# Loading the filter of a long convolution: four transfers of 32 rows spread over all partitions, in place of four into 32 partitions each

## The chip, the cores and the metric

The kernel runs on one core of a Trainium2 chip. Its time is the device time of one execution in microseconds, the median of 3 runs: 234.15 us (233.83 to 234.19).

## The reference, cut to what matters

The output is a sum of three terms over a sequence of S = 2048 positions and D = 640 channels, in bf16:

```
xn  = layernorm(A_q)                                  # along the 640 channels
ks  = 4-tap causal shift filter of k, per channel     # taps: shift_k [640, 4]
kv  = ks * v
y   = causal convolution of kv with ssm_k, per channel   # ssm_k [640, 2048], by FFT of length 4096
y   = y + kv * ssm_D                                  # ssm_D [640]
out = A_q + xn * y + (sigmoid(xn @ w_gate) * (xn @ w_up)) @ w_down     # 640 -> 1728 -> 640
```

In the kernel `h` is the filter `ssm_k`, one row of 2048 taps for each channel, and `D` is `ssm_D`. Since `kv * D` is a convolution with a filter that has D at tap 0 alone, the kernel adds D to tap 0 of h.

## The kernel before, in words

The work has two halves that share the engines. The gated unit runs over 4 groups of 512 positions: `gate` and `up` products (L271) into PSUM, sigmoid on ScalarE (ACT, L280), the multiplication with `up` on VectorE (DVE, L286), and the down projection (L315). The convolution runs over 5 chunks of 128 channels. For each chunk it takes kv and h through a two-stage Fourier transform, multiplies them, and goes back through two inverse stages:

- `load_k`, `load_halo`, `load_v`, `load_taps`, `load_h` bring a chunk in. k with its halo goes to `kx`, v to half 0 of the tile `kvh`, the taps (one row, broadcast to all partitions) to `sraw`, from which `taps` (L155) makes `sc`.
- `h_turn` (L334) turns h with two DVE transposes in blocks of 32 x 32 from the tile `hn` into half 1 of `kvh`. `add_D` (L328, GpSimd) adds D at tap 0. `kv_op` (L348 to L357, DVE) makes kv in half 0.
- `st1_mm` (L374, L376) is the first stage on TensorE, with the table `S1t` as weights; ACT or DVE empties PSUM (`st1_ev`), and `wr1` (L392) writes the result to a DRAM tile `d`. `rd2` (L409) reads it back transposed, `st2_mm` (L418), `prod` and `inv1_mm` (L447) follow; `wr2` and `rdb` (L463, L467, L479) go through DRAM again to `bi`; `inv2_mm` (L488) and `inv2_q` (L493, tile `yx`) finish.

The tile `hn` has 128 partitions and 4 x 512 columns. Partition 32q + r, block k holds the q-th quarter (512 taps) of row 32k + r of the chunk: this is the arrangement from which block transposes give time on the partitions. `hn`, `dr`, `sraw` and `yx` have one buffer each, reused from chunk to chunk. `dr` holds the 128 values of D of one chunk in partition 0.

The order of all work is written out by hand: a string of some 900 letters, each taking the next step of one of about 30 chains. No scheduler changes it, so each engine's instructions, and SyncE's (SP's) transfers, stand in that order. SyncE issues all transfers but three. It waits in order: an issue whose buffer isn't free holds up all that follow. Completions are told by eight semaphores, which the transfers use in turn, so a transfer also waits for the one that had the same semaphore before it. In SyncE's queue, h of chunk 0 stands after the weights w_gate and w_up and before v of chunk 0, the second part of w_down and the table S1t; h of chunk 1 after S1t, and before the second group of x (L133), the taps of chunk 1 (L147) and k of chunk 1.

Of the kernel before, what the change touches and what calls it, by code (L numbers as in the profile page):

```python
# [10 lines left out]
BF16 = mybir.dt.bfloat16  # L11
# [3 lines left out]
ALU = mybir.AluOpType  # L15

S = 2048
DM = 640
FF = 1728
P = 128  # L20
# [37 lines left out]
def kernel(  # L58
# [14 lines left out]
    nc = tc.nc  # L73
# [6 lines left out]
    Drow = A_ssm_D.rearrange("(o d) -> o d", o=1)  # L80
# [7 lines left out]
    res = ctx.enter_context(tc.tile_pool(name="res", bufs=1))  # L88
    cv = ctx.enter_context(tc.tile_pool(name="cv", bufs=1))
    dr = ctx.enter_context(tc.tile_pool(name="dr", bufs=1, space=bass.MemoryType.DRAM))  # L90
# [7 lines left out]
    S1t = res.tile([P, NB, 2, P], U16, name="S1t")  # L98
    TBt = res.tile([P, 2, NB, P], U16, name="TBt")
    SMt = res.tile([P, 3, 32], U16, name="SMt")  # L100
    S1 = S1t.bitcast(BF16)
    TB = TBt.bitcast(BF16)
    SM = SMt.bitcast(BF16)
# [21 lines left out]
    sync = nc.sync  # L125
# [3 lines left out]
    cin = [dict() for _ in range(NC)]  # L129
# [5 lines left out]
    def load_h(c):  # L135

        d = cin[c]
        d["hn"] = cv.tile([P, 4, 512], BF16, name="hn")
        d["dr"] = cv.tile([1, P], BF16, name="dr")
        sync.dma_start(d["dr"][:, :], Drow[:, c * P:(c + 1) * P])  # L140
        for q in range(4):
            src = A_ssm_k[c * P:(c + 1) * P, 512 * q:512 * q + 512].rearrange("(k r) t -> r k t", k=4)
            sync.dma_start(d["hn"][32 * q:32 * q + 32, :, :], src)

    def load_taps(c):
        cin[c]["sraw"] = cv.tile([P, 4 * P], BF16, name="sraw")
        sync.dma_start(cin[c]["sraw"][:], srow[:, 4 * c * P:4 * (c + 1) * P].to_broadcast((P, 4 * P)))  # L147

    def taps(c):
# [175 lines left out]

    def add_D(c):
        h0 = cin[c]["kvh"][0:1, 1, 0:2, :].rearrange("p b c -> p (b c)").rearrange("p (c e) -> p e c", e=2)[:, 0, :]
        nc.gpsimd.tensor_tensor(h0, h0, cin[c]["dr"][:, :], ALU.add)  # L328

    def h_turn(c, n):  # L330

# [27 lines left out]
    chunks = [dict() for _ in range(NC)]  # L359
# [6 lines left out]
    def st1_mm(c, n):  # L366
# [5 lines left out]
        for i in range(4):  # L372
            b = 4 * n4 + i
            nc.tensor.matmul(ps[:, i, 0:P], lhsT=S1[:, b, h, :], rhs=cin[c]["kvh"][:, 0, b, :], start=True, stop=True)  # L374
            hp = cin[c]["kvh"][:, 1, :, :].rearrange("p b c -> p (b c)").rearrange("p (b c e) -> p b e c", b=8, e=2)
            nc.tensor.matmul(ps[:, i, P:2 * P], lhsT=S1[:, b, h, :], rhs=hp[:, b // 2, b % 2, :], start=True, stop=True)  # L376

# [21 lines left out]
    def rd2(s):  # L399
# [5 lines left out]
        else:  # L405
            t2 = (xn[:, 12:NB, :].rearrange("p b d -> p (b d)")[:, 0:2048] if at == 2 else
                  S1[:, 8 * at:8 * at + 8, :, :].rearrange("p b h k -> p (b h k)")).rearrange("p (r e) -> p r e", r=8)
        src = chunks[c]["d1"].rearrange("(r q) h b e -> r (q h b) e", q=NQ)
# [60 lines left out]
    def rdb(c, n):  # L469
# [4 lines left out]
        elif c and n == 1:  # L474
            bi = S1[:, 8:NB, :, :].rearrange("p (h b) s c -> p h (b s) c", h=2)
        else:
# [12 lines left out]
                                 start=(h == 0), stop=(h == 1))  # L489

    def inv2_q(c, m):
        chunks[c]["yx", m] = yx = cv.tile([P, 4, P], BF16, name="yx")
        nc.vector.tensor_tensor(yx[:, :, :], chunks[c]["pb", m][:, :, :], xn[:, 4 * m:4 * m + 4, c * P:(c + 1) * P],  # L493
                                ALU.mult)

# [35 lines left out]
    for i in range(4):  # L531
        m = 3 if i < 3 else NC
# [33 lines left out]
    def hs(c):  # L566
        return [(load_h, c)]
# [7 lines left out]
    for k in ((load_w, sync, 512, 1024, 0),  # L575
              (load_w, sync, 512, 1024, 1),
              (load_taps, 0),
              (sync.dma_start, SMt[:], SMd.ap()),
              (load_w, sync, 1024, 1280, 0),
              (load_w, sync, 1024, 1280, 1),  # L580
              (load_wd, sync, 0, 7),
              *ks(0),
              (load_w, sync, 1280, FF, 0),
              (load_w, sync, 1280, FF, 1),
              *hs(0),
              *vs(0),
              (load_wd, sync, 7, NFC),
              (sync.dma_start, S1t[:], S1d.ap()),
              *hs(1),
              (load_x, sync, 1),  # L590
              *ks(1),
              *vs(1)):
        step("m", *k)
# [4 lines left out]
    for c in range(NC):  # L598
        for n in range(2):
            step("H", h_turn, c, n)  # L600
        step("D", add_D, c)
        for n in range(8):
            step("a", st1_mm, c, n)
# [17 lines left out]
        for m in range(4):  # L621
            step("d", inv2_mm, c, m)
            step("q", inv2_q, c, m)
            step("q", inv2_x, c, m)
        for n in range(16):
            step("k", kv_op, c, n)
        if c == 0:
            continue
        step("T", load_taps, c)
        step("t", taps, c)  # L630
        if c > 1:
# [73 lines left out]
```

## Time and profile before

| what | value |
|---|---|
| median of 3 runs | 234.15 us (233.83 to 234.19) |
| the profiled execution's own time | 234.78 us |
| its span, first to last instruction | 233.0 us |
| granted TensorE clock | 1.000 |
| bytes read from and written to HBM | 36.12 MB, 18.35 MB |
| transfers of h | 20 of 128 KB each |
| one h transfer, issue to landing | 3.4 to 7.7 us, median 5.0 |
| SyncE's time for one such issue | 0.31 to 0.43 us, median 0.42 |

How to read the profile: PE is TensorE, PEld its weight loads, DVE VectorE, ACT ScalarE, POOL GpSimd, SP SyncE (SPq its queue, which issues transfers). L143 is line 143 of the kernel before. A line of the timeline holds start and length in us, engine, line, operation, what is written from what, how many instructions, and in square brackets the engine's idle time before it with what ended it. A line of the stages holds the window, its length, busy time and instructions for PE, PEld, DVE, ACT and POOL, the granted clock, the share of the 16 transfer engines' time that packets took (packets overlap a little, so it can exceed 1), and GB/s. In the rows of ten-digit slices a 9 is 90% or more.

### The profile page before, as it was taken

The numbers are of one execution on the slowest core, as the hardware profiler recorded it, in microseconds if no ns is written. First come the engines' busy times: TensorE is split into PE (matmuls) and PEld (weight loads), VectorE is DVE, ScalarE is ACT, GpSimd is POOL, SyncE is SP. The second block draws the span as 40 slices with busy tenths as digits, with TensorE's granted clock in tenths as the row PEclk, the third lists the DMA queues.
The fourth block names the chain that finished last, engine by engine and source line by source line (L and its number), as shares of the span: only waits on it lengthen the run. The fifth ranks groups of instructions, "written<-read, shape, count | busy, mean of one in ns | idle before, by whom it ended". The sixth has DMA issues, their size and how long they took to land.

```text
span 233.0 us, 5431 instructions
## 1 busy us (share of the span) xinstructions
PE 227.5 (98%) x2199; PEld 130.9 (56%) x2200; DVE 203.4 (87%) x357; ACT 123.5 (53%) x158; POOL 12.4 (5%) x26
## 2 busy tenths in 40 slices
PE   7999999997999999999999999999999999999995
PEld 2844446776454555677554544478654544446772
DVE  5444899799999999999999999997799999997773
ACT  2533321676364887765675847674556667752000
POOL 5210010040001100000011000000000000000000
PEclk9999999999999999999999999999999999999999
DMA  6999999896999969999989899689989999364884
GB/s 199 325 329 208 267 317 294 208 266 143 330 221 303 299 221 242 263 223 230 329 237 277 224 319 272 184 217 190 269 210 311 279 263 254 117 169 117 220 266 136
DMA packets 96159, 56.79 MB, mean 244 GB/s; under 512 B 55878, under 2 KB 90374, under 8 KB 95878
## 3 DMA queue, kind: packets, MB, share of 16 engines
q1 hardware_dynamic: 95702, 56.03, 92.6%
q10 hardware_dynamic: 432, 0.41, 0.5%
q8 instruction: 17, 0.28, 0.5%
q14 instruction: 8, 0.07, 0.1%
HBM read 36.12 MB, written 18.35 MB: 234 GB/s over the span
## 4 chain that ended last, share of the span: by engine, by line
PE 87%; DVE 5%; DMA 4%; issue 1%; SPq 1%; ACT 0%; DVEq 0%
PE pu L271 22%; PE pg L271 22%; PE pd L315 21%; PE psb L488 4%; DMA x<-in_A_q_dram 4%; PE ps L374 3%; PE ps L376 3%; PE ps L418 3%; PE psa L447 2%; PE idle L514 2%; PE pg L292 1%; DVE st L200 1%; PE pg L262 1%; PE pu L262 1%; DVE acc L354 1%
## 5 line engine op out<-in xcount | busy, mean ns | idle before, releaser
L271 PEld LDWEIGHTS <-w 128*128 128x128 bf16 x500 | 46.7, 98 | 53.9 <-issue 4.3
L315 PE MATMUL pd<-wd,hT 128*128 128x320 bf16 (+2 forms) x447 | 65.9, 299 | 0.1
L271 PE MATMUL pu<-xnT,w 128*128 128x512 bf16 x250 | 62.2, 379 | 0.0
L271 PE MATMUL pg<-xnT,w 128*128 128x512 bf16 x250 | 62.2, 379 | 0.0
L315 PEld LDWEIGHTS <-hT 128*128 128x128 bf16 x448 | 41.7, 98 | 18.2 <-issue 2.4
L280 ACT ACTIVATE sig<-pg 128x512 bf16<-128x512 f32 x52 | 31.1, 601 | 30.5 <-PE pg L271 23.8
L286 DVE TENSOR_TENSOR hT<-sig,pu 128x512 bf16<-128x512 bf16 x52 | 35.0, 682 | 10.8 <-PE pu L271 6.9
L232 ACT CAST xz<-ps 128x1024 bf16<-128x1024 f32 x36 | 35.1, 1014 | 15.5 <-PE ps L418 15.5
L232 ACT CAST t<-ps 128x1024 bf16<-128x1024 f32 x24 | 23.8, 1012 | 16.7 <-PE ps L376 14.5
L433 DVE TENSOR_TENSOR xz<-xz 128x2048 bf16<-128x2048 bf16 x20 | 24.4, 1221 | 0.2
L374 PE MATMUL ps<-kvh,S1t 128*128 128x128 bf16 x160 | 21.5, 218 | 1.2 <-DVE kvh L357 1.2
L376 PE MATMUL ps<-kvh,S1t 128*128 128x128 bf16 x160 | 21.6, 220 | 0.0
L354 DVE TENSOR_TENSOR acc<-acc,tmp 128x1024 bf16<-128x1024 bf16 x30 | 20.5, 684 | 0.3
L352 DVE TENSOR_TENSOR tmp<-kx,sc 128x1024 bf16<-128x1024 bf16 x30 | 20.5, 682 | 0.3
L320 DVE TENSOR_TENSOR x<-pd,x 128x320 bf16<-128x320 f32 (+2 forms) x32 | 15.2, 484 | 3.8 <-PE pd L315 3.6
L374 PEld LDWEIGHTS <-S1t 128*128 128x128 bf16 x160 | 15.5, 97 | 3.9 <-DVE kvh L357 1.4
L376 PEld LDWEIGHTS <-S1t 128*128 128x128 bf16 x160 | 15.4, 96 | 2.7 <-issue 0.2
L200 DVE BATCH_NORM_STATS2 st<-x 128x6 f32<-128x320 bf16 x32 | 13.8, 473 | 2.3 <-DMA x<-in_A_q_dram 2.3
L232 ACT CAST TBt<-ps 128x1024 bf16<-128x1024 f32 x14 | 13.8, 1012 | 2.7 <-PE ps L376 2.7
L493 DVE TENSOR_TENSOR yx<-psb,xn 128x512 bf16<-128x512 f32 x20 | 13.7, 687 | 1.4 <-PE psb L488 0.8
L431 DVE STREAM_SHUFFLE xz<-xz 128x512 f32<-128x512 f32 x20 | 14.6, 729 | 0.0
L232 ACT CAST ao<-psa 128x1024 bf16<-128x1024 f32 x9 | 9.0, 1013 | 8.6 <-PE psa L447 6.9
(56 smaller groups left out, 159.2 us busy)
## 6 DMA issues: line engine op xcount, KB each, us to landing
t<-d SPq DMA_DIRECT2D x15, 512.0 KB, 6.0
d<-t SPq DMA_DIRECT2D x13, 512.0 KB, 4.1
d<-TBt SPq DMA_DIRECT2D x7, 512.0 KB, 5.9
d<-ao SPq DMA_DIRECT2D x6, 512.0 KB, 5.5
bi<-d SPq DMA_DIRECT2D x6, 512.0 KB, 5.4
kx<-in_A_k_dram SPq DMA_DIRECT2D x10, 256.0 KB, 5.8
hn<-in_A_ssm_k_dram SPq DMA_DIRECT2D x20, 128.0 KB, 5.0
kvh<-in_A_v_dram SPq DMA_DIRECT2D x10, 256.0 KB, 5.2
```

The source lines that it names most:

```text
L200: nc.vector.bn_stats(st[:, i, SD * s2:SD * s2 + SD], x[:, b, s2 * 320:(s2 + 1) * 320])
L232: nc.scalar.copy(out=out, in_=in_)
L271: nc.tensor.matmul(pg[:, :], lhsT=w[:, c, u * UP + fc * P:u * UP + (fc + 1) * P], rhs=xnT[:, :, c, :], start=(c == 0), stop=(c == NC - 1))
L280: nc.scalar.activation(sig[fc][:, :], pgs[0, fc][:, :], ACT.Sigmoid)
L286: nc.vector.tensor_tensor(hT[:, fc, :], sig[fc][:, :], pgs[1, fc][:, :], ALU.mult)
L315: nc.tensor.matmul(pd[:, :], lhsT=hT[:, fc, bb * P:(bb + 1) * P], rhs=wd[:, fc, es], start=(fc == 0), stop=(fc == NFC - 1))
L320: nc.vector.tensor_tensor(x[:, 4 * t + bb, es], pds[bb, half][:, :], x[:, 4 * t + bb, es], ALU.add)
L352: nc.vector.tensor_tensor(d["tmp"][:, :, :], kx[:, lo + 3 - m:hi + 3 - m, :], sb(m), ALU.mult)
L354: nc.vector.tensor_tensor(d["acc"][:, :, :], d["acc"][:, :, :], d["tmp"][:, :, :], ALU.add)
L374: nc.tensor.matmul(ps[:, i, 0:P], lhsT=S1[:, b, h, :], rhs=cin[c]["kvh"][:, 0, b, :], start=True, stop=True)
L376: nc.tensor.matmul(ps[:, i, P:2 * P], lhsT=S1[:, b, h, :], rhs=hp[:, b // 2, b % 2, :], start=True, stop=True)
L433: nc.vector.tensor_tensor(z[:, 1:3, :, :], z[:, 0:1, :, :].to_broadcast((P, 2, 8, P)), z[:, 1:3, :, :], ALU.mult)
```

## The change

Each chunk's h still comes in four transfers of 128 KB, but they are cut the other way. Before, transfer q brings one quarter of the taps of all 128 rows into the 32 partitions of that quarter. After, transfer k brings all 2048 taps of 32 rows into block k of all 128 partitions. Both move 128 pieces of 1024 bytes. On the source side the new transfer steps over q (4), r (32) and 512 taps.

D comes once, 640 values into one row that stays (`Dt`), in place of 128 values a chunk. The room in SBUF for it is made by letting `sraw` and `yx`, which have the same size, share one buffer (`tag="sy"`). Nothing else changes; the engines' instructions and their order are the same.

```diff
+    Dt = res.tile([1, DM], BF16, name="Dt")
...
     def load_h(c):
 
         d = cin[c]
+        if c == 0:
+            sync.dma_start(Dt[:, :], Drow[:, :])
         d["hn"] = cv.tile([P, 4, 512], BF16, name="hn")
-        d["dr"] = cv.tile([1, P], BF16, name="dr")
-        sync.dma_start(d["dr"][:, :], Drow[:, c * P:(c + 1) * P])
-        for q in range(4):
-            src = A_ssm_k[c * P:(c + 1) * P, 512 * q:512 * q + 512].rearrange("(k r) t -> r k t", k=4)
-            sync.dma_start(d["hn"][32 * q:32 * q + 32, :, :], src)
+        for k in range(4):
+            r0 = c * P + 32 * k
+            sync.dma_start(d["hn"][:, k, :], A_ssm_k[r0:r0 + 32, :].rearrange("r (q t) -> q r t", q=4))
 
     def load_taps(c):
-        cin[c]["sraw"] = cv.tile([P, 4 * P], BF16, name="sraw")
+        cin[c]["sraw"] = cv.tile([P, 4 * P], BF16, name="sraw", tag="sy")
...
     def add_D(c):
...
-        nc.gpsimd.tensor_tensor(h0, h0, cin[c]["dr"][:, :], ALU.add)
+        nc.gpsimd.tensor_tensor(h0, h0, Dt[:, c * P:(c + 1) * P], ALU.add)
...
     def inv2_q(c, m):
-        chunks[c]["yx", m] = yx = cv.tile([P, 4, P], BF16, name="yx")
+        chunks[c]["yx", m] = yx = cv.tile([P, 4, P], BF16, name="yx", tag="sy")
```

## The prediction

> **What bounds the kernel now.** I read the page first (shares, slices, chain), then the queue of SyncE in order of time, then who waits around the h loads.
>
> ```profile
> span 233.0 us, 5431 instructions
> ...
> PE 227.5 (98%) x2199; PEld 130.9 (56%) x2200; DVE 203.4 (87%) x357; ACT 123.5 (53%) x158; POOL 12.4 (5%) x26
> ...
> DMA  6999999896999969999989899689989999364884
> ...
> PE 87%; DVE 5%; DMA 4%; issue 1%; SPq 1%; ACT 0%; DVEq 0%
> ```
>
> TensorE is busy nearly throughout and carries 87% of the chain, so a transfer costs time only where its landing holds up TensorE, directly or through DVE or ACT. But the transfer engines have no idle stretch either before 190 us (nines in the DMA row), so extra time there is passed on to what is queued behind. The stages, with the DMA share and GB/s last in each line:
>
> ```profile
> 22.00:30.00 8.00, 8.00 (x39) 3.61 (x38) 6.93 (x11) 2.28 (x4) 0.00 (x0) 1.00 1.12 255
> 30.00:36.00 6.00, 6.00 (x30) 2.71 (x28) 5.93 (x9) 1.79 (x3) 0.78 (x1) 1.00 1.11 352
> 36.00:46.00 10.00, 10.00 (x92) 7.47 (x91) 8.29 (x16) 3.87 (x5) 0.00 (x0) 1.00 0.96 241
> ```
>
> From 22 to 46 us, where the h of chunks 0 and 1 is loaded, the share is about 1: the queue never runs dry. SyncE's order there, and the consumers:
>
> ```profile
> 22.76 1.76 SPq L143 DMA_DIRECT2D hn<-in_A_ssm_k_dram x4
> ...
> 33.67 1.75 SPq L143 DMA_DIRECT2D hn<-in_A_ssm_k_dram x4
> 35.46 1.29 SPq L133 DMA_DIRECT2D x<-in_A_q_dram  x1
> 36.80 0.43 SPq L147 DMA_DIRECT2D sraw<-in_A_shift_k_dram  x1
> ```
>
> ```profile
> 42.79 1.11 DVE L334 STREAM_TRANSPOSE kvh<-hn 128x512 f32<-128x512 f32 x1 [1.15 <-DMA hn<-in_A_ssm_k_dram]
> 44.29 0.89 DVE L200 BATCH_NORM_STATS2 st<-x 128x6 f32<-128x320 bf16 x2 [0.39 <-DMA x<-in_A_q_dram]
> ```
>
> ```profile
> 44.75 0.66 ACT L155 COPY sc<-sraw 128x512 bf16<-128x512 bf16 x1 [1.07 <-DMA sraw<-in_A_shift_k_dram]
> 45.31 1.91 ACT L232 CAST t<-ps 128x1024 bf16<-128x1024 f32 x2
> ```
>
> The reader should see that h of chunk 1, the x group behind it and the taps (sraw) behind that are each awaited already. There is no slack at 42.8 to 44.8 us, and ACT empties PSUM (`t<-ps`) for TensorE's next first-stage matmuls (46.1 us) only after the taps.
>
> **The change, part by part.** The program's order shows the same instructions in the same order on TensorE, DVE, ACT and GpSimd; only SyncE's transfers differ.
>
> *h now.* The four transfers of chunk 0 are issued from 22.76 to 24.09 us and take 4.8 to 5.3 us to land: landings at 27.55, 28.15, 28.73, 29.37, a step of 0.61 us with a full queue. Each is 128 rows of 1024 B, 8 an engine on 16 engines, so 76 ns a row. The weight load of 640 KB (40 rows of 1024 B an engine) landed 1.87 us after the one before it, 47 ns a row. So h now pays 4 x 0.61 = 2.4 us a chunk on all engines, with slow rows. [...]
>
> *h after: how many engines.* The trace records each engine's completion as a semaphore increment. Transfers whose outermost step counts 128, 112, 64 or 32 get 16 landings; the 15-row halo (L164) gets 15, and one increment within 0.2 us of its issue; the D row (L140, one row) gets a single landing. The engines used follow the outermost count. After the change the destination's outermost count is 128, but the source's is 4 (the quarters q; then 32 rows of 512). No transfer here has such a pair; the nearest, the read-back of `bi` (128 against 256), is on 16. The bounds are 4 and 16 engines. I take 4, since a small outermost count has cut the engines each time it occurred. [...]
>
> *Price.* On 4 engines a transfer is 32 rows an engine: 32 x 47 ns = 1.5 us, 6.0 us a chunk, 3.6 us more than now on those four engines (the other twelve get nothing). Bounds: 8 x 47 ns = 0.4 us on 16 engines, 0.8 us a chunk less; or 32 rows at today's 76 ns, 9.7 us a chunk, 7.3 more. I keep 47 ns, the row of transfers into all partitions. Whatever is queued behind waits for its share on the four engines.
>
> *Chunk 0.* Last landing 29.37 + 3.6 = 33.0 us; the DVE transpose L334 started at 30.12, so DVE stands for 2.9 us, with the product L357 and the `up` multiplications L286 behind it, which free PSUM for TensorE. The v load, w_down and S1t (awaited at 40.5 us, landed 39.98) follow in the queue. This isn't added, since the next wait contains it.
>
> *Chunk 1.* With the queue never dry, the 3.6 us of chunk 0 are still there: 7.2 us on four engines. Today one straggling engine sets the landings: x has 15 landings by 42.6 (mean 41.6) and the last at 44.27; h means 39.8 and the last at 42.66; sraw 42.3 and 44.65. If the straggler isn't one of the four, these become 7.2 on top of the means: h 47.0 (+4.3), x 48.8 (+4.5), sraw 49.5 (+4.8). DVE and ACT wait for these with under 0.15 us of slack, and TensorE for ACT. I take **4.5 us**, chunk 0's share included.
>
> *Chunks 2 to 4*, each 3.6 us later against today's slack. Chunk 2: landed 69.42, transpose at 72.14, so 0.9 late; the v half behind it landed 73.57, needed from 75.06, so 2.1 late on DVE. Chunk 3: 92.44 against 96.02, just covered. Chunk 4: 112.14 against 119.68, covered; behind it the write of `d` lands at 116.96 and ACT needs its buffer from 119.2 to 120.6: 0 to 1.4 late. Together 0.9 to some 4; I take **2.4 us**, the middle.
>
> *Issue.* An issue whose sides have different outermost counts (`bi`, L479) took 0.53 us against 0.42 for h: 0.11 x 20 = 2.2 us of SyncE, 0.44 a chunk. Hidden by the backlog; bounds 0 to 0.4. SyncE itself was held in single issues up to 2.67 us (18.36) when some 130 rows an engine were outstanding; the four h transfers now bring 128 on four engines, so what follows is issued later, but it would have waited in the queue anyway: 0.
>
> *D.* Four issues fewer (0.26, 0.23, 0.91, 0.39 us) and no wait for GpSimd before chunk 1 (1.6 us); but h behind it waits for the DVE transpose that ends at 33.64, and started at 33.67 already. 0; at best -0.4. The completion semaphores, eight in turn, are dealt differently: the 1.5 us for which the last h of chunk 2 waited for x falls to the read L409, issued 2 us after that landing: 0.
>
> *sraw and yx in one buffer.* The last copy out of sraw is at 109.5, the first yx (L493) at 145.9: 36 us of cover, 0.
>
> **Sum.** 4.5 + 2.4 = 6.9 us. The profiled execution took 234.78 us (span 233.0 and 1.8 around); so 241.7 beside it, and 234.15 + 6.9 = **241.0** on the median, from which the profiled run stands 0.6 up.
>
> **Rivals.** *1, sixteen engines: not slower.* The rows run at 47 ns and each chunk frees 0.8 us of queue. For it: destination of 128 partitions, and 76 ns now. Against: no transfer in the trace kept 16 engines with a small outermost count. What it could gain is TensorE's 1.2 us wait at 55.2 for DVE, late since 42.79; up to 0.8 of it, less where the straggler sets the landing: 233.3 to 234.3, say 233.7. It decides if an h transfer shows 16 landings. *2, four engines, mostly hidden.* The straggler's 2 to 2.7 us and gaps at 50 us (TensorE and DVE before the transposed loads) absorb all but some 2.5 us: 236.6. Against: the waits under 0.15 us at 42.8 to 44.8. *3, four engines and worse.* Rows at 56 ns, between 47 and 76, make 4 x 32 x 56 ns - 2.4 = 4.8 us a chunk: 9.6 less the 2.7 that the straggler hides (7.2 - 4.5) = 6.9 for the first two chunks, 2.4 + 3 x 1.2 = 6.0 for the rest: 247; a straggler among the four adds 2.0 instead (243 to 249).
>
> **Chances.** Forecast, 5 to 9 us more: 0.50. Rival 1: 0.20, of it 0.07 faster, 0.10 within 0.2% (0.47 us, about what a measurement of this kernel can tell from no change) and 0.03 slower. Rival 2: 0.14. Rival 3: 0.16. The range 233.9 to 248 leaves out the faster part of rival 1 and the end of rival 3, some 0.15; the forecast's own range is 239 to 243. Faster 0.07, same 0.10, slower 0.83.
>
> **What would show it.** Each h transfer with one increment at issue and four landings, and four in a row landing 1.5 us apart; to-landing of h from 5.0 up to 8 or more; the DVE waits before L334 and L200 of chunk 1 grown from 1.15 and 0.39 to some 5 together, ACT's before L155 likewise, and a TensorE gap near 46 us; packets of 1024 B at 47 ns. Wrong, if h shows sixteen landings, or if h lands late and TensorE has no new gap.

## The result and the profile after

| | us, median | runs |
|---|---|---|
| kernel before | 234.34 | 6, from 233.83; one stray run of 336.42 |
| changed kernel | 243.69 | 6, from 243.27 to 246.18 |

The ratio is 1.043 (95% interval 1.037 to 1.049), taken without the stray run; by the medians of the table the changed kernel is 9.35 us slower, 9.5 us without that run. The profiled execution of the changed kernel took 243.77 us, with a span of 242.0 us and a granted clock of 1.000. Line numbers of the changed kernel are those of the kernel before plus 1. The page:

```profile
span 242.0 us, 5426 instructions
...
PE 229.3 (95%) x2199; PEld 131.4 (54%) x2200; DVE 203.5 (84%) x357; ACT 123.2 (51%) x158; POOL 12.5 (5%) x26
...
DMA  6999678899878997889899999969999899654884
...
PE 49%; DMA 22%; SPq 15%; DVE 9%; issue 3%; ACT 2%; DVEq 0%; ACTq 0%
```

The engines do the same work as before (TensorE 229.3 us busy for 227.5, DVE 203.5 for 203.4). TensorE's share of the chain that ended last fell from 87% to 49%; transfers and SyncE's queue now hold 37% of it. The dips in the DMA row are new: the queue has work, but not for all transfer engines. The same three stages as in the prediction (DMA share and GB/s last):

```profile
22.00:30.00 8.00, 8.00 (x39) 3.64 (x38) 6.54 (x12) 2.39 (x4) 0.00 (x0) 1.00 0.73 208
30.00:36.00 6.00, 6.00 (x30) 2.69 (x28) 3.42 (x5) 1.19 (x2) 0.77 (x1) 1.00 0.74 204
36.00:46.00 10.00, 8.40 (x68) 5.68 (x67) 8.53 (x14) 3.21 (x4) 0.00 (x0) 1.00 0.97 270
```

The share was 1.12, 1.11 and 0.96 before. SyncE's order in that stretch is unchanged, but it stands in single issues:

```profile
22.74 3.19 SPq L144 DMA_DIRECT2D hn<-in_A_ssm_k_dram  x4
25.98 4.06 SPq L174 DMA_DIRECT2D kvh<-in_A_v_dram  x2
30.08 2.60 SPq L187 DMA_DIRECT2D wd<-in_B_w_down_dram  x1
...
36.72 2.25 SPq L144 DMA_DIRECT2D hn<-in_A_ssm_k_dram  x4
```

The four issues of h took 1.76 us before, and now 3.19 and 2.25. Chunk 1's begin at 36.72, where they began at 33.67, since the buffer `hn` waits for chunk 0's second transpose. In the semaphore records each h transfer now shows one early increment (0.9 to 1.5 us after its issue begins in sixteen of the twenty, 2.3 to 2.8 in four) and then four landings. From issue to last landing it takes 4.9 to 9.4 us, in the median 6.9. The last landings of chunk 0 are at 28.30, 29.95, 31.37 and 33.06 us, a mean step of 1.59; those of chunk 1 at 41.94, 44.33, 46.36 and 47.79, a mean step of 1.95.

Who waits, in the timelines of DVE, ACT and TensorE:

```profile
33.18 1.10 DVE L335 STREAM_TRANSPOSE kvh<-hn 128x512 f32<-128x512 f32 x1 [2.54 <-DMA hn<-in_A_ssm_k_dram]
...
47.91 1.10 DVE L335 STREAM_TRANSPOSE kvh<-hn 128x512 f32<-128x512 f32 x1 [3.23 <-DMA hn<-in_A_ssm_k_dram]
49.48 0.89 DVE L201 BATCH_NORM_STATS2 st<-x 128x6 f32<-128x320 bf16 x2 [0.46 <-DMA x<-in_A_q_dram]
```

```profile
50.00 0.64 ACT L156 COPY sc<-sraw 128x512 bf16<-128x512 bf16 x1 [4.04 <-DMA sraw<-in_A_shift_k_dram]
50.55 1.92 ACT L233 CAST t<-ps 128x1024 bf16<-128x1024 f32 x2
```

```profile
37.92 1.24 PE L293 MATMUL pg<-xnT,w 128*128 128x512 bf16 x5 [1.60 <-DMA wd<-in_B_w_down_dram]
51.61 0.22 PE L375 MATMUL ps<-kvh,S1t 128*128 128x128 bf16 x1 [2.94 <-ACT t L233]
60.43 0.23 PE L375 MATMUL ps<-kvh,S1t 128*128 128x128 bf16 x1 [1.14 <-DVE kvh L358]
```

The second TensorE line is the chain of the forecast: x and the taps are late, ACT empties PSUM only after the taps, and TensorE stands for 2.94 us before the first-stage matmul. Ahead of it there is a wait of 1.60 us that the forecast had folded into this one. The view puts it down to w_down, but these matmuls don't read w_down. Their matmul instruction waits for DVE's semaphore, and DVE ends a multiplication with `up` at 37.86, 0.05 us before the matmul starts:

```profile
37.19 0.67 DVE L287 TENSOR_TENSOR hT<-sig,pu 128x512 bf16<-128x512 bf16 x1
```

So this wait, too, comes from h of chunk 0: DVE stood 2.54 us for it at 33.18 and reached its multiplications late. The third wait, 1.14 us, is for DVE's product kv, behind the late h of chunk 1. The profile before has such a wait at the same matmul:

```profile
55.24 0.23 PE L374 MATMUL ps<-kvh,S1t 128*128 128x128 bf16 x1 [1.20 <-DVE kvh L357]
```

A comparison of these two profiles therefore doesn't show it. The experiments below left nine other profiles in which chunk 1's h runs on eight or sixteen engines, and none of them has this wait.

To see where TensorE falls behind, its weight loads can be matched one to one between the two profiles. The changed kernel runs 0.4 us late before L293, 2.2 after it, 5.25 at the first-stage matmul at 51.61, and still 5.2 at 111 us. It then loses more at the second-stage matmul L419 (5.9 at 117 us) and at the gate matmul L272 (7.7 at 132 us), and ends 9.0 late. So about 5.2 us are lost by chunks 0 and 1, nothing that shows by chunk 2, and 3.7 us while chunks 3 and 4 come in. Against the profile of the kernel with h alone undone (first experiment below), which has no wait at the third place, the delay is 5.1 us at 51.61 and 6.3 behind 60.43. The profiled execution of the kernel before stood 0.4 us above its median here, and 0.6 to 1.0 above the medians of the larger sets below, so differences against it come out short.

### The profile page after: what moved, and what is told of

It reads as the page before. It is cut to its first block, busy times and chain, and to the rows that moved or that the text cites. A ratio compares the mean times of both kernels' runs of the same rounds, so it can differ in the third digit from the quotient of the medians.

```text
span 242.0 us, 5426 instructions
## 1 busy us (share of the span) xinstructions
PE 229.3 (95%) x2199; PEld 131.4 (54%) x2200; DVE 203.5 (84%) x357; ACT 123.2 (51%) x158; POOL 12.5 (5%) x26
## 4 chain that ended last, share of the span: by engine, by line
PE 49%; DMA 22%; SPq 15%; DVE 9%; issue 3%; ACT 2%; DVEq 0%; ACTq 0%
PE pd L316 16%; PE pu L272 11%; PE pg L272 10%; DMA hn<-in_A_ssm_k_dram 7%; PE psb L489 4%; DMA sraw<-in_A_shift_k_dram 4%; DMA kvh<-in_A_v_dram 3%; DMA kx<-in_A_k_dram 3%; DMA d<-ao 3%; PE ps L419 3%; SPq L178 2%; DMA t<-d 2%; SPq L144 2%; SPq L393 2%; DVE kvh L335 2%
## 5 line engine op out<-in xcount | busy, mean ns | idle before, releaser
L272 PEld LDWEIGHTS <-w 128*128 128x128 bf16 x500 | 46.7, 98 | 55.7 <-issue 6.2
L272 PE MATMUL pg<-xnT,w 128*128 128x512 bf16 x250 | 62.2, 379 | 1.6 <-ACT sig L281 1.6
L272 PE MATMUL pu<-xnT,w 128*128 128x512 bf16 x250 | 62.2, 379 | 0.0
L281 ACT ACTIVATE sig<-pg 128x512 bf16<-128x512 f32 x52 | 31.1, 601 | 30.5 <-PE pg L272 23.3
L335 DVE STREAM_TRANSPOSE kvh<-hn 128x512 f32<-128x512 f32 x10 | 10.9, 1102 | 6.4 <-DMA hn<-in_A_ssm_k_dram 6.4
```

The source lines that it names most:

```text
L272: nc.tensor.matmul(pg[:, :], lhsT=w[:, c, u * UP + fc * P:u * UP + (fc + 1) * P], rhs=xnT[:, :, c, :], start=(c == 0), stop=(c == NC - 1))
L281: nc.scalar.activation(sig[fc][:, :], pgs[0, fc][:, :], ACT.Sigmoid)
L335: nc.vector.transpose(to[:, 4 * n:4 * n + 4, :, :], hv[:, 4 * n:4 * n + 4, :, :])
```

## The experiments

**Which part of the change, and how many engines.** Four kernels on one chip, against 234.03 us of the kernel before (233.46 to 235.62, 25 runs). The first undoes the h part alone and keeps D in one transfer and the shared buffer:

```diff
-        for k in range(4):
-            r0 = c * P + 32 * k
-            sync.dma_start(d["hn"][:, k, :], A_ssm_k[r0:r0 + 32, :].rearrange("r (q t) -> q r t", q=4))
+        for q in range(4):
+            src = A_ssm_k[c * P:(c + 1) * P, 512 * q:512 * q + 512].rearrange("(k r) t -> r k t", k=4)
+            sync.dma_start(d["hn"][32 * q:32 * q + 32, :, :], src)
```

> The changed kernel with h loaded as before (four transfers into 32 partitions each); D in one transfer and the shared buffer of sraw and yx stay. Theory (the loss is all from h on four engines): 233.7 to 234.8 us, the time of before, and sixteen landings for each h transfer. Rival (the other transfers of D, the semaphores dealt differently or the shared buffer carry a part): 235 us or more.

Measured: 234.02 us, ratio 1.0005 (0.998 to 1.003). Each h transfer has sixteen landings again. D in one transfer and the shared buffer cost and bring nothing that can be measured; the loss is h's.

The other three keep a destination of all 128 partitions and pieces of 1024 bytes, and differ from one another in the source's outermost count alone. A transfer of theirs reads 512 taps of 128 rows, where the change reads 2048 taps of 32 rows, and brings them to other partitions, so the filter is not the reference's; the amount of work is the same.

```diff
-            r0 = c * P + 32 * k
-            sync.dma_start(d["hn"][:, k, :], A_ssm_k[r0:r0 + 32, :].rearrange("r (q t) -> q r t", q=4))
+            src = A_ssm_k[c * P:(c + 1) * P, 512 * k:512 * k + 512].rearrange("(b a) t -> a b t", a=16)   # a=8, a=2
+            sync.dma_start(d["hn"][:, k, :], src)
```

Sixteen:

> Each h transfer again fills block k of all 128 partitions with 128 rows of 1024 B, but the source steps over 16 outermost and 8 inner rows (the rows land in other places, so the convolution's filter is not the reference's; the amount of work is the same). Theory (the source's outermost count sets the engines): sixteen landings, 8 rows an engine at about 47 ns, 0.4 us a transfer, 233.3 to 234.4 us. Rival (writing one block of 128 partitions, or a source of two steps, is slow by itself): 240 us or more.

Eight:

> As the kernel with sixteen outermost steps, with 8 outermost and 16 inner rows (the filter's rows again land in other places). Theory: eight landings and one increment at issue; 16 rows an engine at 50 to 58 ns, 0.8 to 0.95 us a transfer against 0.61 before, some 1 us more a chunk on eight engines, most of it under what slack there is: 234.3 to 236.5 us. Rival (count of engines doesn't matter): the same time as with sixteen.

Two:

> As the kernel with sixteen outermost steps, with 2 outermost and 64 inner rows. Theory: two landings and one increment at issue; 64 rows an engine at 50 to 58 ns, 3.2 to 3.7 us a transfer, 13 to 15 us a chunk against 2.4 before and some 6.7 in the changed kernel: some 6 to 8 us more a chunk than the changed kernel, nearly all exposed, 270 to 283 us. Rival (the engines' count doesn't matter): no slower than the changed kernel, 243.7 us.

| source's outermost count | landings of an h transfer | step in chunk 0, us | time, us | ratio (95%) |
|---|---|---|---|---|
| 16 | 16 | 0.46 | 233.65 | 0.997 (0.995 to 0.999) |
| 8 | 8 | 0.96 | 234.38 | 1.002 (0.999 to 1.004) |
| 4 (the change, from the result above) | 4 | 1.59 | 243.69 | 1.043 (1.037 to 1.049) |
| 2 | 2 | 2.90 | 268.24 | 1.146 (1.139 to 1.153) |

The number of engines is the source's outermost count in all four, and it carries the whole loss: with sixteen, the transfer into all partitions is a little better than the kernel before. Its step of 0.46 us is 57 ns a row, above the expected 47. Eight engines take twice as long for an h, and the time still doesn't change: what covers a late h ends between 1.0 and 1.6 us a transfer. With two, step and time came out below what was expected (3.2 to 3.7 us, 270 to 283 us). The 268.24 us are not the price of the engines alone: the granted clock of these four executions was only 0.936 to 0.961. With two engines alone at work, their rate can be read from the GB/s row (slices of 0.8 us from 22 to 54 us):

```profile
GB/s 153 375 372 365 149 36 46 46 45 46 46 45 46 70 227 144 47 116 258 40 69 161 381 395 394 316 379 420 216 46 46 46 46 46 46 46 45 155 243 378
```

46 GB/s on two engines is 23 GB/s each, or 1024 bytes in 45 ns; the step of 2.90 us over 64 rows says the same. That is the price of a row when the other engines are empty.

**Which chunks.** Here some chunks load h as the change does and the others as before (`if c < 2:` and so on around the two loops); D and the buffer are as in the change. The first four kernels ran against 233.79 us of the kernel before (233.44 to 234.81, 7 runs).

> The changed kernel, but chunks 2 to 4 load h as before; only chunks 0 and 1 go in four transfers on four engines. Theory A (the loss comes at two places: TensorE's delay grew by about 5.2 us up to the first-stage matmul L375 of chunk 1, and by 3.7 us after 111 us): 234.0 + 5.2 = 239.2 us, between 238.5 and 240.0, and together with the run of chunks 2 to 4 alone the two losses add up to the 9.3 us of the whole change. Theory B (the two places are one: a late start leaves the later chunks less cover): more than 5.2 is left here or less there, and the two don't add up.

> The changed kernel, but chunks 0 and 1 load h as before; chunks 2 to 4 go in four transfers on four engines. Theory A: 234.0 + 3.7 = 237.7 us, between 237.0 and 238.5, with h of chunk 2 late but TensorE not (in the changed kernel its delay didn't grow there) and the loss at the copy of sraw of chunk 4 (L156) and the gate matmuls behind it. The prediction's step gave 2.4 (236.4). Theory B (the transfers' dates hang on the queue, not on TensorE, so that without the 5.2 us at the start TensorE reaches these loads earlier than they land): 239 or more.

> The changed kernel, but only chunk 0 loads h in four transfers on four engines, the others as before. Theory A (backlog on four engines, carried on in a queue that isn't dry, and covered in part by the one engine that lands 2 to 2.7 us after the others before chunk 1): 3.3 to 4 us of backlog, of which the straggler covers up to 2.7; the wait for w_down at L293 grows from about 0 to 1.6 us as in the changed kernel: 235.3 to 236.2. Rival (no cover, each chunk carries half of the 5.2): 236.6.

> The changed kernel, but only chunk 1 loads h in four transfers on four engines, the others as before. Theory A: 4 us of backlog less the straggler's 2.7: 235.3 to 236.0, the two runs of one chunk together 2 us or more short of the 5.2 of both. Rival (no cover): 236.6, and the two add up.

The run of the last three chunks led to three kernels with one of them each, run against 234.16 us (233.41 to 235.34, 35 runs):

> The changed kernel, but only chunk 2 loads h in four transfers on four engines, the others as before. The prediction's step: DVE 0.9 to 2.1 us late, so 234.7 to 235.9. Rival, from the changed kernel's trace, where TensorE's delay didn't grow at this place: within 0.5 us of the kernel before, 233.6 to 234.4; DVE is late, but does other work before TensorE needs what hangs on it.

> The changed kernel, but only chunk 3 loads h in four transfers on four engines, the others as before. The prediction's step: just covered, 0, so within 0.5 us of the kernel before, 233.5 to 234.4. Rival, from the run of the last three chunks, where TensorE's delay grew by about 1.8 us at 111 to 112 us (L424, for a cast by DVE), before h of chunk 4 was issued: then this comes from chunk 3, 235.3 to 236.0.

> The changed kernel, but only chunk 4 loads h in four transfers on four engines, the others as before. The prediction's step: the write of d behind it lands late, 0 to 1.4 us, so 233.8 to 235.2, and SyncE's being held in issue costs nothing. Rival: SyncE is held in the four issues (4.0 us in the changed kernel against 1.75) and the small transfers of the transforms behind it (the reads t<-d, xn<-d and the writes d<-t), which need no bandwidth but start at once in the kernel before, are late by that and by the rows in front of them on the four engines: 1.8 to 2.5 us, 235.6 to 236.4, with ACT's wait for the write d<-t at 125 us at 3 us or more.

| chunks on four engines | time, us | over before | ratio (95%) |
|---|---|---|---|
| 0 and 1 | 240.40 | 6.6 | 1.028 (1.025 to 1.032) |
| 2, 3 and 4 | 237.94 | 4.15 | 1.016 (1.013 to 1.020) |
| 0 | 236.18 | 2.4 | 1.011 (1.007 to 1.015) |
| 1 | 236.80 | 3.0 | 1.013 (1.010 to 1.016) |
| 2 | 234.63 | 0.5 | 1.002 (1.000 to 1.003) |
| 3 | 236.20 | 2.0 | 1.009 (1.006 to 1.012) |
| 4 | 234.13 | 0.0 | 1.000 (0.998 to 1.003) |

What follows, by theory. Theory A's split stands for the later chunks (237.94 in 237.0 to 238.5). For the first two it was low (240.4 against at most 240.0). The two halves sum to 10.8 against 9.35 for the whole. With intervals of some 0.8 us to either side on each half and 1.3 on the whole, this does not tell whether they add up. Two things in the traces bear on it. The 5.2 us of theory A leave out the third wait above, 1.1 to 1.2 us. And in the run of the first two chunks the granted clock fell after TensorE's long wait, there 3.22 us:

```profile
51.50:57.50 6.00, 5.91 (x32) 4.09 (x32) 5.90 (x15) 4.10 (x6) 2.49 (x4) 0.50 1.19 261
```

It was 0.50 in this stretch (the third number from the right), where the changed kernel's profile has 1.00 after a wait of nearly the same length. TensorE was 5.2 us late at its start, as in the changed kernel, and 7.9 at its end, with no wait between; 6.7 were left when the place of the third wait was passed, and here there was none. The four executions' mean clock was 0.986 to 0.993, so part of the 6.6 us is the clock's; how much of the median is not shown.

Chunk 1 alone went against theory A: it cost 3.0 us rather than 1.5 to 2.2, close to the 2.8 expected if nothing covered it. Its profile has the forecast's chain by itself, with ACT held by the taps and TensorE by ACT, and the third wait behind it:

```profile
46.92 0.64 ACT L161 COPY sc<-sraw 128x512 bf16<-128x512 bf16 x1 [2.90 <-DMA sraw<-in_A_shift_k_dram]
47.47 1.92 ACT L238 CAST t<-ps 128x1024 bf16<-128x1024 f32 x2
```

```profile
48.52 0.22 PE L380 MATMUL ps<-kvh,S1t 128*128 128x128 bf16 x1 [1.80 <-ACT t L238]
57.41 0.23 PE L380 MATMUL ps<-kvh,S1t 128*128 128x128 bf16 x1 [1.21 <-DVE kvh L363]
```

The two waits make 3.0 us. (These kernels' lines are those of the kernel before plus 6; h is issued at L145 or, as before, at L149.) The cover that theory A counted on is the late engine of the profile before, and that profile was an unlucky one: its last landing of the taps is 1.6 us behind the last but one, at 44.65. In the seven other profiles where chunks 0 and 1 load h on sixteen engines, that lag is 0.0 to 1.3 us and the taps are there at 42.4 to 44.1. So there is less to hide behind in most executions. Why one engine lags is open.

Chunk 0 alone, at 236.18, lies at the upper end of theory A. TensorE's one long wait there is the first of the three, and here the view itself names DVE:

```profile
38.39 2.19 PE L298 MATMUL pg<-xnT,w 128*128 128x512 bf16 x5 [2.07 <-DVE hT L292]
```

Chunks 0 and 1 alone sum to 5.4, only 1.2 short of the two together, and that is inside the noise.

*Chunk 2.* At 234.63 us it lies between the two expectations, just under 234.7 to 235.9 and above 233.6 to 234.4; 0.5 us is at the edge of what can be told from no change.

*Chunk 3, and who carries it.* The prediction had it just covered. Alone it cost 2.0 us, at 236.20 a little more than the rival's 235.3 to 236.0. SyncE's queue in that kernel:

```profile
85.71 3.75 SPq L145 DMA_DIRECT2D hn<-in_A_ssm_k_dram  x4
...
94.06 3.30 SPq L415 DMA_DIRECT2D t<-d  x1
97.47 3.09 SPq L256 DMA_TRANSPOSE xnT<-xn  x1
...
106.84 0.63 SPq L153 DMA_DIRECT2D sraw<-in_A_shift_k_dram  x1
```

and in the kernel before:

```profile
87.35 1.76 SPq L143 DMA_DIRECT2D hn<-in_A_ssm_k_dram  x4
...
92.70 1.01 SPq L409 DMA_DIRECT2D t<-d  x1
93.82 2.81 SPq L250 DMA_TRANSPOSE xnT<-xn  x1
...
103.41 0.60 SPq L147 DMA_DIRECT2D sraw<-in_A_shift_k_dram  x1
```

SyncE started on h 1.6 us earlier and was done with it 0.35 us later; the issues behind it took longer (the read `t<-d` 3.30 us for 1.01), and it is 3.65 us late at the transposed loads and 3.4 at the taps of chunk 4. That looks like the cause, but the waits say something else. DVE, then TensorE:

```profile
97.43 2.11 DVE L340 STREAM_TRANSPOSE kvh<-hn 128x512 f32<-128x512 f32 x2 [2.04 <-DMA hn<-in_A_ssm_k_dram]
...
110.87 1.22 DVE L241 CAST t<-ps 128x1024 bf16<-128x1024 f32 x1
```

```profile
112.14 0.44 PE L424 MATMUL ps<-t,SMt 32*32 32x512 bf16 x16 [1.40 <-DVE t L241]
```

In the kernel before, the two transposes start at 96.02 and that cast at 109.47. Both are 1.4 us later here, and TensorE waits 1.40 us. DVE has no idle time between the two, so what its wait of 2.04 us before the transposes cost it arrives at TensorE 15 us later. The last h had landed at 97.24, 4.8 us later than the 92.44 of before, where the forecast counted on 3.6 with a slack of 3.58. It is one engine that is so late: the other three had landed at 95.23, 95.24 and 95.80, and DVE stood from 95.39 on. The late taps are there too, but TensorE is released by DVE, not by ACT.

*Chunk 4, alone and behind chunk 3.* Alone it costs nothing, so the rival that put 1.8 to 2.5 us on SyncE's hold there is out: its h issues took 2.56 us in place of 1.75, and TensorE lost nothing by what stood behind. With chunks 2 and 3 on four engines as well, the same issues start 4.8 us later. First SyncE with chunk 4 alone, then SyncE and ACT with chunks 2 to 4:

```profile
105.06 2.56 SPq L145 DMA_DIRECT2D hn<-in_A_ssm_k_dram  x4
...
115.97 1.21 SPq L398 DMA_DIRECT2D d<-t  x1
```

```profile
109.82 3.57 SPq L145 DMA_DIRECT2D hn<-in_A_ssm_k_dram  x4
...
120.22 2.12 SPq L398 DMA_DIRECT2D d<-t  x1
```

```profile
124.83 1.01 ACT L238 CAST t<-ps 128x1024 bf16<-128x1024 f32 x1 [3.40 <-DMA d<-t]
```

The write `d<-t` goes out 4.25 us later, where TensorE is only some 2 us later, and ACT stands 3.40 us for it; TensorE loses 1.6 us between 124 and 132 us. This fits the difference between 4.15 us for chunks 2 to 4 together and 2.5 for the three run singly: chunk 3's hold of SyncE makes chunk 4's h late. No run tried it by itself, so it is read from the trace, not shown by a run.

**Is there a version that beats both?** h in four transfers of 32 partitions as before, in another order:

```diff
+        for q in (0, 2, 1, 3):
+            src = A_ssm_k[c * P:(c + 1) * P, 512 * q:512 * q + 512].rearrange("(k r) t -> r k t", k=4)
+            sync.dma_start(d["hn"][32 * q:32 * q + 32, :, :], src)
```

> Not a test of the loss but of what could be better than both: h as before in four transfers of 32 partitions on sixteen engines, with the quarters in the order 0, 2, 1, 3 instead of 0, 1, 2, 3 (D in one transfer, as in the changed kernel). [...] If each transfer is limited by itself, or by its own 32 partitions: no change, 233.6 to 234.2.

Measured: 233.80 us, ratio 0.999 (0.997 to 1.001). It can't be told from the kernel before. The transfers do land a little closer together, at a mean step of 0.55 and 0.53 us in chunks 0 and 3, against 0.58 to 0.67 in the other profiles with these chunks' h as before; the time doesn't show it. The kernel with sixteen in the source is the only one that is faster with an interval clear of 1, by 0.26%, and it puts the rows on other partitions than the block transposes of this kernel are laid out for.

## Why the prediction was right, and where it was short

The forecast was 241.0 us and the result 243.69: right in sign and mechanism and in the wide range, but 0.7 above the forecast's own range of 239 to 243 and inside that of rival 3 (243 to 249).

- *How many engines: right.* One early increment, four landings; and 16, 8 and 2 landings where the source's outermost count is 16, 8 and 2. With four, the transfer engines' busy share was 0.28 at 94 GB/s while little but h was under way (29.5 to 30.5 us; four of sixteen are 0.25), and with two the rate was 46 GB/s: some 23 GB/s for each landing. The destination's count is 128 in all four; what another count on that side does with such a source, no run shows.
- *Price of a transfer: too low, and the main term that was mis-sized.* 1.5 us was taken, from 47 ns a row; measured 1.59 in chunk 0, 1.95 in chunk 1 and about 1.7 to 1.8 in chunks 2 to 4, 50 to 61 ns a row. The 47 ns came from one load of weights on all sixteen engines. A row of h took 57 ns on sixteen and 60 on eight; only the two engines that worked alone had 45. The value of rival 3, 56 ns, was nearer, and its 247 us overshot about as much as the forecast fell short.
- *Chunk 0: right landing, wrong bookkeeping.* The last h landed at 33.06 (33.0 forecast) and DVE stood 2.54 us (2.9). It reached TensorE by the way that was forecast, the `up` multiplications behind it. But it was not contained in the next wait: TensorE lost 1.60 us at L293, and chunk 0 alone costs 2.4 us.
- *Chunk 1: right chain, sizes short.* h at 47.79, x at 49.45, taps at 49.90, against 47.0, 48.8 and 49.5. ACT's wait grew from 1.07 to 4.04 us, and DVE's two came to 3.7, for some 5. TensorE's loss by these two chunks was 5.2 us against the profile before, 6.3 against that of the kernel with h alone undone, and 6.6 by their run, for 4.5. Two things failed. The 2.7 us of cover by the straggler were read from one profile, which has the longest lag of all. And that profile has TensorE's wait of 1.2 us at 55.24, which the forecast took to be part of every execution: it is part of the price of a late h of chunk 1, and was not in the sum.
- *Chunks 2 to 4: 2.4 us forecast, 3.7 by the traces and 4.15 by their run, and in other places.* Chunk 2 cost 0.5 for 0.9 to 2.1; chunk 4 alone 0.0 for up to 1.4; and chunk 3, put at 0, cost 2.0. That the sum came within 2 us is partly luck, since the first two were put too high and the third too low. For chunk 3 a landing forecast at 96.0 was set against a need at 96.02: a slack that the price just fills was costed at nothing. Three engines then filled it, landing at 95.2 to 95.8, and the fourth, at 97.24, broke it.
- *SyncE held in issue: 0 was too low, though not where it looks largest.* In chunks 0 and 1 it may well cost nothing: in the packet records at least four packets are under way on average in every half microsecond from 26 to 50 us, so it looks as if the four engines, which set the dates, were never left without rows. The other twelve were, and the share fell to 0.73. No run tried this by itself. The 2.67 us that the forecast took for the longest hold before was not the longest: the read at 176.30 was held for 3.77. With the small transfers of the transforms behind it, the hold of chunk 3 makes chunk 4's write late, by the reading above up to 1.6 us.
- *Issue of unlike sides: right.* 0.53 us was taken from `bi`, and the median of the 20 h issues is 0.59 with four engines and 0.60 with eight or sixteen, so with four to sixteen engines it goes with the shape and not with their number. It was hidden: the kernel with sixteen pays it and is faster.
- *D, the shared buffer: right,* 1.0005.
- *Rival 1 (sixteen engines, 233.7): its condition failed, its price came out right, by luck.* Given sixteen engines the time is 233.65. But the price was read from TensorE's wait at 55.24, and the kernel with h alone undone doesn't have that wait in its profile either, and takes 234.02 us. An h transfer into all partitions on sixteen engines takes 0.46 us in place of 0.61. That is a factor of 1.3 a transfer; whether the partitions or the source's shape bring it, no run shows. On this kernel's path it is worth 0.4 us. *Rival 2 (mostly hidden, 236.6)* fell with the cover that it relied on.

## What to carry to other kernels

Before cutting a transfer another way, write down the outermost count of both sides: here 4 in the source against 128 in the destination took twelve engines away, and cost more than twenty times what the transfer into all partitions on sixteen engines brought (9.35 against 0.4 us). Price a row by rows that run beside the traffic it will run beside, and don't cost at nothing a landing whose slack is just as long as the delay. Before you count on a late engine as cover, or take a wait for a fixed part of the kernel, see whether a second profile has it. When an engine is late and busy without a gap, look for the wait far ahead: here DVE carried 1.4 us over 15 us of work to TensorE.

## What the runs showed that was not expected

- A row of 1024 bytes took 45 ns where two engines worked alone, and 50 to 61 ns on four engines beside other traffic. Why is open; no run separated the source side from the partitions.
- Half the engines are free of cost here: eight, with 0.96 us a transfer, give 1.002 (0.999 to 1.004), while four give 1.043. On this kernel fewer engines cost nothing until the cover is used up.
- The granted clock can take part in such a loss: it was 0.50 from 51.5 to 57.5 us in the run of the first two chunks, after TensorE had waited 3.22 us, and 0.936 to 0.961 over the whole of the kernel with two engines. After the changed kernel's wait of 2.94 us it stayed at 1.00.
- SyncE's time for one h issue grows as the engines get fewer: the longest is 1.33 us with sixteen, 1.47 with eight, 2.26 with four and 3.39 with two. With two the median is 1.39, where the shortest is 0.50.
- The order 0, 2, 1, 3 of the four transfers into 32 partitions, in place of 0, 1, 2, 3, makes no difference to the time (0.999, 0.997 to 1.001), though the transfers land a little closer together (0.53 to 0.55 us for 0.58 to 0.67).
